# A row of transfers in another order: exchange a pair ahead, two pairs fetched into room of late outputs, the second pair first (hash attention and feed-forward, one core)

## The chip, the cores and the metric

The kernel runs on one core of a Trainium2 chip. The core has TensorE (PE) for matrix products, VectorE (DVE), ScalarE (ACT) and GpSimd (POOL) for elementwise work, and SyncE (SP), which here only issues transfers (DMA). All share an on-chip memory, SBUF; PE writes its sums to PSUM. The metric is the device time of one execution in microseconds (us), the median of several; less is better.

## The reference

Two blocks follow one another. The first is attention in which a query sees only keys with the same hash; the second is a feed-forward with a GELU.

```python
# q, k, v: (4, 8, 768, 64) f32; proj: (64, 6); x: (3072, 512); w_in: (512, 2048); w_out: (2048, 512)
q_bits = (np.einsum('bhsd,dk->bhsk', q, proj) > 0)       # 6 bits; the same for k
mask = q_bucket[:, :, :, None] == k_bucket[:, :, None, :]
scores = np.where(mask, scale * np.matmul(q, k.transpose(0, 1, 3, 2)), -1e9)
attn = softmax(scores)                                    # rows
x = np.matmul(attn, v)  -> (B*S, H*D)
h = x @ w_in
out = (h * (1.0 / (1.0 + np.exp(-1.702 * h)))) @ w_out
```

## The kernel before, in words

**Tiling of the attention.** Two heads of one batch make a *pair*; there are 16 pairs (0 to 15). A head has 64 columns, so a pair fills 128 partitions. The 768 queries are halved (c = 0, 1; 384 each), and the 768 keys are six tiles of 128 (kt). For a half and a key tile PE makes scores in a PSUM place (`place`, four of them in turn, `in_turn`), ACT writes their exponentials into `es[c]` (`weigh`, L486), POOL and DVE add them up over the key tiles (`add_low`, L525, into one shared `low_sum`; `add_high`, L535 and L538), and PE multiplies them with the values (`values`, L547). ACT moves that into `xT` (`unload`, L558 and L559), and two half-pairs later DVE multiplies by the inverse of the sums (`total` on PE, L569; `invert`; `norm`, L590).

**The mask.** It is no comparison but a second term in the scores. `hashed` (L461) multiplies keys and queries with the projection, DVE writes one tile `f` of signed bits (`featured`, L466), and eight transfers (two of them from ACT in pair 1) bring its parts of 16 rows into the feature tile `feats` of the pair (two tiles, used in turn). Score terms are thus: features, in bf16, and keys by queries in f32.

**Two forms of the score product.** Pairs 0 to 2 (`n < BY_PARTS`, 3) use `scores` (L497): for each key tile and head a product over 64 rows for each term. Later pairs use `scores_of_four` (L514): four products over 32 rows run side by side, for two key tiles and two heads. That needs, beside the pair's own keys and queries (`own`, three in turn), a copy with the 32-row halves of each head exchanged (`other`, written by the four transfers of `exchange`), and the features twice, 32 rows apart (two transfers inside the feature tile). `spread` issues these six.

**Loading.** `fetch` brings keys or queries of a pair into one tile each (`ld` pool, one buffer of each name), in four transfers of 32 partitions, so that a 32 by 32 transposition on DVE (`turn`, L437) makes `own` of it. `measure` (L451) takes the sum of squares of the raw tile on ACT. A fetch of a later pair can start only when both have read the tile. `fetch_v` brings values in two transfers, with two buffers. Pair 0 is special (`first_pair`): loaded by SP and ACT, transposed by PE, with its bits taken by products of their own (L416, L417).

**What sets the order.** The lists of PE, DVE, ACT and POOL run as written. All transfers above are issued by SP, which works its list in order (its rows bear L340, the line of `load`): a transfer that waits holds up all behind it. Up to pair 1 a scheduler may place SP's transfers; from pair 2 on (`turns_kept`) they, too, keep the written order. ACT issues the chunks of w_in (one for each pair from 2 on, `begin`, L165), which DVE and ACT convert in steps (`step`). Behind pair 15 the feed-forward begins (L905, L973, L1232).

The order of a middle pair n on SP is: eight feature transfers of pair n+1, four of `exchange(n + 1)`, two inside the feature tile, four keys of pair n+3, two values of n+1, four queries of n+3:

```python
whole(features)
if n + 1 >= BY_PARTS:
    spread(n + 1)
...
fetch(n + 3, "k")     # behind turn(n + 2, "k") and measure(n + 2, "k")
fetch_v(n + 1)
...
fetch(n + 3, "q")     # behind turn(n + 2, "q") and measure(n + 2, "q")
```

Of the kernel before, what the change touches and what calls it, by code (L numbers as in the profile page):

```python
# [19 lines left out]
P = 128  # L20
# [18 lines left out]
def kernel(  # L39
# [249 lines left out]
    def attention(ff):  # L289
# [4 lines left out]
        with actx:  # L294
# [34 lines left out]
            BY_PARTS = 3  # L329
# [7 lines left out]
            turns_kept = [False]  # L337

            def load(out, in_):
                dma = nc.sync.dma_start(out=out, in_=in_)  # L340
                if turns_kept[0]:
                    tc.keep_in_program_order(dma)
                return dma
# [6 lines left out]
            def behind(x):  # L350

                nc.vector.memset(x, 0.0)
# [14 lines left out]
            def fetch_v(n):  # L367
                b, hp = pairs[n]
                x = ld.tile([P, T, 2, D], F32, tag="v", name="v", bufs=2)
                if n == 0:  # L370
                    x = x.rearrange("p t j d -> p (t j d)").rearrange("p (j t d) -> p t j d", j=2, d=D)
                vts[n] = x
                if n == 1:
                    behind(x[:, 0, :, 0])
                for j in range(2):
                    order = "(t p) d -> p t d" if n else "(p t) d -> p t d"
                    load(x[:, :, j, :], v[b, 2 * hp + j].rearrange(order, p=P))

            def first_pair():
# [16 lines left out]
                for _ in range(4):  # L396
                    nc.tensor.matmul(warm[:, 0], idle[:, 0:P], idle, start=True, stop=True)
# [15 lines left out]
                def bits(name, c, slots=None):  # L413
                    cols = slice(c * HS, (c + 1) * HS)
                    h = (place(slots.pop(0)) if slots else in_turn())[:, 0, 0:HS]
                    nc.tensor.matmul(h, pf0[name].rearrange("p j d -> p (j d)"), xts[0, name][:, cols], start=True, stop=True)  # L416
                    nc.vector.tensor_scalar(feats[0][name][:, cols], h, above0[name][:, 0:1], FEAT[name],  # L417
                                            op0=Alu.is_gt, op1=Alu.mult)
# [60 lines left out]
            def spread(n):  # L479

                exchange(n)
# [6 lines left out]
            def scores(n, c, kts, slots=None):  # L488
                qT, kT, qf, kf = xts[n, "q"], xts[n, "k"], feats[n % 2]["q"], feats[n % 2]["k"]
                cols = slice(c * HS, (c + 1) * HS)  # L490
                for kt in kts:
                    ps = in_turn() if slots is None else place(slots.pop(0))
                    keys = slice(kt * P, (kt + 1) * P)
                    for a, m, last in ((kf, qf, False), (kT, qT, True)):
                        for j in range(2):
                            hs = slice(D * j, D * (j + 1))
                            nc.tensor.matmul(ps[:, j, 0:HS], a[hs, keys], m[hs, cols], start=not last, stop=last)  # L497
                    weigh(n, c, kt, ps)

            def scores_of_four(n, groups):  # L500

                for c, k0 in groups:
# [6 lines left out]
                    for at, (a, m) in enumerate(((f["k"], f["q"]), (x[:, 0], x[:, 1]), (y[:, 0], y[:, 1]))):  # L509
# [30 lines left out]
            def values(n, c, kts, at):  # L540
                av, vt = at[:, 0 : HS + 1], vts[n]
                avs[n, c] = av
                for t in kts:
                    row = t if n else 2 * (t % GT) + t // GT
                    for j in range(2):
                        for d in range(0, D, 32):
                            nc.tensor.matmul(av[D * j + d : D * j + d + 32, :], vt[:, row, j, d : d + 32], es[c][:, t, j, :],  # L547
# [44 lines left out]
            last = len(pairs) - 1  # L592
# [29 lines left out]
            scores(0, 0, low, slots)  # L622
            rest(slots)
            add_low(0, 0)
            scores(0, 0, high, slots)
            turn(1, "k")
            measure(1, "k")
            values(0, 0, low, at[:, 0])
            fetch(2, "k")
            scores(0, 1, low, slots)  # L630
            turn(1, "q")
# [877 lines left out]
```

## Time and profile before

| what | us |
|---|---|
| median of 3 runs | 855.31 (854.36 to 855.37) |
| the profiled execution, its own time | 857.29 |
| its span, first to last instruction | 855.5 |
| attention, to the first product of the feed-forward | 0 to 317.4 |
| ACT busy with exponentials (192) | 143.7 |
| PE busy with products by the values (1536) | 131.6 |

The rows of the profile name the line, the engine, the operation and the tiles it writes and reads, `out<-in`; in a timeline the first number is the start and the second the length in us, xN is how many instructions are merged in the row, and brackets give the idle time before it and what ended it. A queue's own rows (SPq, ACTq) are issues of transfers; their length includes what the issue waited for. "Landing" is from the issue of a transfer to its end.

### The profile page before, as it was taken

The numbers are of one execution on the slowest core, as the hardware profiler recorded it, in microseconds if no ns is written. First come the engines' busy times: TensorE is split into PE (matmuls) and PEld (weight loads), VectorE is DVE, ScalarE is ACT, GpSimd is POOL, SyncE is SP. The second block draws the span as 40 slices with busy tenths as digits, with TensorE's granted clock in tenths as the row PEclk, the third lists the DMA queues.
The fourth block names the chain that finished last, engine by engine and source line by source line (L and its number), as shares of the span: only waits on it lengthen the run. The fifth ranks groups of instructions, "written<-read, shape, count | busy, mean of one in ns | idle before, by whom it ended". The sixth has DMA issues, their size and how long they took to land.

```text
span 855.5 us, 14892 instructions
## 1 busy us (share of the span) xinstructions
PE 843.9 (99%) x5595; PEld 524.7 (61%) x5595; DVE 683.9 (80%) x1069; ACT 337.6 (39%) x553; POOL 361.8 (42%) x321
## 2 busy tenths in 40 slices
PE   8999999999999999999999999999999999999997
PEld 4444444444444444565666666545888888888886
DVE  4479889988878986788887788676998977897786
ACT  6666665667666644343444444433000000000000
POOL 4333343433433448997854467568664100000000
PEclk9999999999999999999999999999999999999999
DMA  5657866776777403526466546577854675467534
GB/s 112 98 91 150 152 137 134 158 138 130 155 146 142 114 3 135 161 81 264 188 230 221 214 155 213 205 265 269 278 174 154 205 244 194 157 222 233 193 120 100
DMA packets 165197, 144.04 MB, mean 168 GB/s; under 512 B 124384, under 2 KB 139872, under 8 KB 159872
## 3 DMA queue, kind: packets, MB, share of 16 engines
q1 hardware_dynamic: 154640, 111.22, 47.6%
q10 hardware_dynamic: 10480, 31.81, 11.8%
q8 instruction: 45, 0.74, 0.4%
q14 instruction: 32, 0.26, 0.1%
HBM read 79.69 MB, written 50.33 MB: 152 GB/s over the span
## 4 chain that ended last, share of the span: by engine, by line
PE 89%; SPq 3%; DMA 3%; ACT 1%; DVE 1%; issue 1%; POOL 1%; ACTq 0%; DVEq 0%; POOLq 0%
PE product L1232 30%; PE product L905 23%; PE s L547 12%; PE s L514 12%; PE small L973 6%; SPq L340 3%; PE product L973 3%; DMA feat<-feat 1%; PE s L497 1%; DMA q<-in_q_dram 1%; ACT e L486 1%; PE s L569 1%; PE s L461 1%; DVE acc L538 0%; POOL above L334 0%
## 5 line engine op out<-in xcount | busy, mean ns | idle before, releaser
L486 ACT ACTIVATE e<-s 128x768 f32<-128x768 f32 x192 | 143.7, 812 | 62.2 <-PE s L514 46.6
L547 PE MATMUL s<-e,v 128*32 128x385 f32 x1536 | 131.6, 488 | 0.0
L525 POOL TENSOR_TENSOR t_x<-e 128x768 f32<-128x768 f32 x32 | 55.2, 1724 | 137.5 <-ACT e L486 132.0
L905 PE MATMUL product<-xT,w_in_sb 128*128 128x512 f32 x216 | 100.0, 593 | 0.1
L547 PEld LDWEIGHTS s<-e,v 128*32 128x32 f32 x1536 | 47.2, 109 | 79.1 <-issue 60.3
L905 PE MATMUL product<-t_x,s_in 128*128 128x512 f32 x192 | 89.5, 593 | 0.0
L514 PE MATMUL s<-s_in 32*128 32x384 f32 x816 | 79.9, 482 | 0.0
L525 POOL TENSOR_TENSOR t_x<-t_x,e 128x768 f32<-128x768 f32 x32 | 55.9, 1747 | 55.7 <-ACT e L486 54.6
L538 DVE TENSOR_TENSOR acc<-acc,e 128x768 f32<-128x768 f32 x63 | 73.6, 1168 | 2.8 <-ACT e L486 0.6
L1268 ACT COPY u<-product 128x256 f32<-128x256 f32 x20 | 7.4, 372 | 158.1 <-PE product L1232 124.9
L905 PEld LDWEIGHTS product<-xT,w_in_sb 128*128 128x128 f32 x216 | 41.0, 190 | 35.7 <-issue 32.7
L905 PEld LDWEIGHTS product<-t_x,s_in 128*128 128x128 f32 x192 | 36.5, 191 | 29.8 <-issue 26.7
L514 PEld LDWEIGHTS s<-s_in 32*128 32x128 f32 x816 | 41.1, 185 | 19.8 <-issue 1.9
L514 PE MATMUL s<-own 32*128 32x384 f32 x432 | 45.6, 487 | 0.0
L921 DVE TENSOR_TENSOR u<-product,u 128x256 f32<-128x256 f32 (+1 forms) x60 | 28.4, 486 | 15.5 <-PE product L973 12.9
L466 DVE TENSOR_SCALAR f<-s,above,weight 128x384 bf16<-128x384 f32 x15 | 10.1, 676 | 32.9 <-PE s L569 25.0
L1232 PE MATMUL product<-raw_g,xT 128*128 128x256 f32 x152 | 35.1, 380 | 0.0
L514 PE MATMUL s<-feat 32*128 32x384 bf16 x312 | 30.4, 327 | 2.5 <-DMA feat<-feat 2.0
L226 POOL TENSOR_TENSOR v<-c,v 128x1024 f32<-128x1024 f32 (+1 forms) x15 | 32.3, 2156 | 1.0
L225 POOL TENSOR_TENSOR u<-v,u 128x1024 f32<-128x1024 f32 (+1 forms) x11 | 23.8, 2166 | 20.2 <-ACT v L918 14.1
L921 DVE TENSOR_TENSOR v<-product,v 128x512 f32<-128x512 f32 x24 | 16.5, 689 | 19.5 <-PE product L905 19.5
L535 DVE SCALAR_TENSOR_TENSOR acc<-t_x,e 128x768 f32<-128x768 f32 x31 | 29.4, 947 | 3.1 <-ACT e L486 2.5
(298 smaller groups left out, 1801.1 us busy)
## 6 DMA issues: line engine op xcount, KB each, us to landing
raw_g<-g_dram SPq DMA_DIRECT2D x20, 1024.0 KB, 5.1
s_in<-g_dram SPq DMA_DIRECT2D x20, 1024.0 KB, 5.0
g_dram<-c ACTq DMA_DIRECT2D x18, 512.0 KB, 2.9
raw<-in_moe_w_out_dram ACTq DMA_DIRECT2D x16, 512.0 KB, 3.7
raw<-in_moe_w_in_dram ACTq DMA_DIRECT2D x15, 512.0 KB, 5.2
s_in<-own SPq DMA_DIRECT2D x36, 192.0 KB, 3.3
v<-in_v_dram SPq DMA_DIRECT2D x32, 192.0 KB, 3.8
k<-in_k_dram SPq DMA_DIRECT2D x60, 96.0 KB, 3.1
```

Source lines behind the costliest of these rows:

```text
L226: lambda: eng.tensor_tensor(b12, b22, b12, op=Alu.subtract),
L340: dma = nc.sync.dma_start(out=out, in_=in_)
L486: nc.scalar.activation(es[c][:, kt, :, 0:HS], ps[:, :, 0:HS], Act.Exp, scale=1.0 / D**0.5)
L514: nc.tensor.matmul(ps[i][:, j, 0:HS], a[r0 : r0 + 32, keys], m[r0 : r0 + 32, cols], start=at == 0, stop=at == 2)
L525: nc.gpsimd.tensor_tensor(low_sum, low_sum if i else e[:, 0], e[:, i + 1], op=Alu.add)
L535: nc.vector.scalar_tensor_tensor(acc, terms[0], T * TINY, terms[1], op0=Alu.add, op1=Alu.add)
L538: nc.vector.tensor_tensor(acc, acc, terms[i + 1], op=Alu.add)
L547: nc.tensor.matmul(av[D * j + d : D * j + d + 32, :], vt[:, row, j, d : d + 32], es[c][:, t, j, :], start=(t == 0), stop=(t == T - 1))
L905: nc.tensor.matmul(ps, wq[LEFT[i]][:, kc, :], xq[RIGHT[i]][:, kc, :], start=(start and kc == 0), stop=(kc == K2 - 1), skip_group_check=not ...
L921: nc.vector.tensor_tensor(dst, x, y, op=Alu.add)
L973: nc.tensor.matmul(x, wq[LEFT[i]], xq[RIGHT[i]], start=start, stop=True, skip_group_check=True)
L1232: nc.tensor.matmul(ps, wq[LEFT[i]][:, c, :], gq[RIGHT[i]][:, c, :], start=(onto is None and c == 0), stop=(c == F4 - 1), skip_group_check= ...
```

## The change

- **Row of a middle pair on SP.** `exchange` leaves `spread`, which becomes `copied` (the two transfers inside the feature tile). For pair n+2 (not n+1) it is issued at the end of pair n's row, behind the query fetch. `copied(n + 1)` comes behind the key fetch and ahead of the values. Values are one transfer (tile order p, j, t, d; was p, t, j, d). All of SP's transfers keep the written order from the start.
- **Room.** Keys and queries of pairs 1 and 3 are fetched into the parts of `xT` that pairs 14 and 13 write at their end, instead of into the tiles of the `ld` pool.
- **Forms.** `BY_PARTS` is 2: pair 2 also has 32-row products. Pair 0's scores begin with the f32 term.
- **Pairs 0 and 1.** One more warm-up product. In `first_pair` the second halves' bits come behind the first three key tiles, as one piece (`second`). The fetches of pairs 1, 2, 3 and 4 come earlier, and the values of pair 0 behind the fetch of pair 1. The hash of pair 2 and the sums of pair 0 (`total`) come ahead of pair 1's scores, and its features right behind; pair 1 leaves the loop and is written out: all scores of its first half, all of its second, then the values of the first.

```diff
-            BY_PARTS = 3
+            BY_PARTS = 2
...
             def load(out, in_):
-                dma = nc.sync.dma_start(out=out, in_=in_)
-                if turns_kept[0]:
-                    tc.keep_in_program_order(dma)
-                return dma
+                return tc.keep_in_program_order(nc.sync.dma_start(out=out, in_=in_))
...
                 b, hp = pairs[n]
-                x = raws[n, name] = ld.tile([P, S // 32, 32], F32, tag=name, name=name)
-                if (n, name) == (2, "q"):
-                    behind(x[:, 0, 0:1])
+                if n in (1, 3):
+
+                    b1, hp1 = pairs[last - 1 - "kq".index(name)]
+                    x = xT[:, hp1, b1 * S : (b1 + 1) * S].rearrange("p (s i) -> p s i", i=32)
+                else:
+                    x = ld.tile([P, S // 32, 32], F32, tag=name, name=name)
+                raws[n, name] = x
...
-                x = ld.tile([P, T, 2, D], F32, tag="v", name="v", bufs=2)
+                x = vts[n] = ld.tile([P, 2, T, D], F32, tag="v", name="v", bufs=2)
+                heads = v[b, 2 * hp : 2 * hp + 2]
+                if n:
+                    load(x.rearrange("p j t d -> p (j t) d"), heads.rearrange("j (t p) d -> p (j t) d", p=P))
...
-                for _ in range(4):
+                for _ in range(5):
...
                 placed("k", tk, 0, (act, act))
                 tq = turned("q")
+                placed("q", tq, 0, (act, dve))
+                bits("k", 0, in_turn()[:, 0])()
                 placed("k", tk, 1, (act, dve))
-                placed("q", tq, 0, (act, dve))
-                bits("k", 0)
-                bits("q", 0)
-                measure(0, "k")
-                placed("q", tq, 1, (act, act))
-                bits("k", 1)
-                measure(0, "q")
-                return lambda slots: bits("q", 1, slots)
+                bits("q", 0, in_turn()[:, 0])()
+                placed("q", tq, 1, (act, dve))
+
+                def second():
+                    at = place(3)
+                    for f in [bits(x, 1, at[:, i]) for i, x in enumerate("kq")]:
+                        f()
+
+                return second
...
-            def spread(n):
-
-                exchange(n)
+            def copied(n):
+
                 for j in range(2):
                     load(both[n % 2][D * j + 32 : D * j + 48], both[n % 2][D * j : D * j + 16])
...
             rest = first_pair()
-            fetch_v(0)
             for x in "kq":
                 fetch(1, x)
+            fetch_v(0)
             slots = [2, 0, 1] * 5
+            scores(0, 0, low, slots)
+            measure(0, "k")
+            fetch(2, "k")
+            rest()
+            measure(0, "q")
+            fetch(2, "q")
+            add_low(0, 0)
...
+            fetch_v(1)
+            for x in "kq":
+                fetch(3, x)
             scores(0, 1, low, slots)
...
             whole(featured(1))
-            fetch(2, "q")
-            fetch_v(1)
             scores(0, 1, high, slots)
-            measure(2, "k")
+            for x in "kq":
+                turn(2, x)
+                measure(2, x)
+            exchange(2)
+            add_high(0, 1)
             at = place(3)
             values(0, 1, every, at[:, 0])
+            hashed(2, at[:, 1])
             unload(0, 1)
-            turns[0] = 0
-            inverse = {}
-            for n in range(1, last + 1):
+            at = place(0)
+            total(0, at[:, 0])
+            turns[0] = 1
+
+            features = featured(2)
+            next(features)
+            inverse = {0: invert(0)}
+            next(inverse[0])
+            whole(features)
+            for x in "kq":
+                fetch(4, x)
+            scores_of_four(1, ((0, 0), (0, 2), (0, 4)))
+            add_low(1, 0)
+            copied(2)
+            for x in "kq":
+                turn(3, x)
+            fetch_v(2)
+            exchange(3)
+            add_high(1, 0, (0, 1))
+            next(inverse[0])
+            scores_of_four(1, ((1, 0), (1, 2), (1, 4)))
...
+            for x in "kq":
+                measure(3, x)
+            at = in_turn()
+            values(1, 0, every, at[:, 0])
+            hashed(3, at[:, 1])
+            unload(1, 0)
+            for n in range(2, last + 1):
...
+                if n + 3 <= last:
+                    fetch(n + 3, "k")
                 if n < last:
+                    copied(n + 1)
                     fetch_v(n + 1)
...
                 if more:
-                    measure(n + 2, "k" if n == 1 else "q")
-                    if n > 1 and n + 3 <= last:
+                    measure(n + 2, "q")
+                    if n + 3 <= last:
                         fetch(n + 3, "q")
+                    exchange(n + 2)
```

More of the change, by code (lines that the diff above doesn't have):

```diff
@@ new lines, in attention @@
+            add_high(1, 0, (0, 1))
+            next(inverse[0])
+            scores_of_four(1, ((1, 0), (1, 2), (1, 4)))
+            add_low(1, 1)
+            norm(0)
+            add_high(1, 0, (2,))
+            for x in "kq":
+                measure(3, x)
[4 more added lines that the diff above has]
+            for n in range(2, last + 1):
+                more = n + 2 <= last
+                if n == last:
+                    turns[0] += 1
+                if n < last:
+                    features = featured(n + 1)
+                    next(features)
+                if n > 2:
+                    inverse[n - 2] = invert(n - 2)
+                    next(inverse[n - 2])
+                    step(n - 1, 2 if n == last else 1)
+                scores_of_four(n, ((0, 0),))
+                chunk = begin(n)
+                if n < last:
+                    first = next(features)
+                    if chunk is not None:
+                        behind_issue(chunk, first)
+                        behind_issue(next(features), chunk)
+                    whole(features)
+                scores_of_four(n, ((0, 2),))
@@ L689, in attention @@
                 add_high(n - 1, 1, (2,))
[L690 removed]
+                if n > 2:
                     norm(n - 2)
[L692 to L705 removed]
+                if more:
+                    measure(n + 2, "k")
@@ L713, in attention @@
                 add_high(n, 0, (1,))
-                if n > 1 and more:
+                if more:
                     turn(n + 2, "q")
-                elif n + 1 == last:
+                elif n < last:
                     x_sums[1]()
```

118 lines of the change are left out of this document (26 added, 92 removed).

## Prediction

> **What bounds the kernel now.** I read the page's first and fourth parts first, then the busy time of each pair's stretch, and last the timeline of SyncE (SP) around the longest wait of TensorE (PE).
>
> ```profile
> span 855.5 us, 14892 instructions
> PE 843.9 (99%) x5595; PEld 524.7 (61%) x5595; DVE 683.9 (80%) x1069; ACT 337.6 (39%) x553; POOL 361.8 (42%) x321
> PE 89%; SPq 3%; DMA 3%; ACT 1%; DVE 1%; issue 1%; POOL 1%; ACTq 0%; DVEq 0%; POOLq 0%
> ```
>
> PE is the bound: 99% busy, and 89% of the chain that ended last. What the chain has beside PE is mostly SP and transfers, 3% each. A PE row that is held up still counts as busy, so the page's busy time understates the waits; the length of a pair shows them better. I took each pair from its first score product to that of the next (pair 1 starts at 29.55, pair 2 at 45.96, pair 3 at 66.62, pair 12 at 239.16):
>
> ```profile
> 29.55:45.96 16.41, 16.41 (x149) 8.64 (x146) 9.63 (x10) 12.48 (x20) 6.47 (x4) 1.00 0.80 124
> 45.96:66.62 20.66, 20.07 (x188) 8.78 (x185) 17.22 (x20) 13.35 (x24) 6.58 (x4) 1.00 0.60 116
> 66.62:85.94 19.32, 19.17 (x236) 8.69 (x232) 17.12 (x25) 12.45 (x21) 6.77 (x4) 1.00 0.78 144
> ...
> 142.17:163.37 21.20, 19.18 (x236) 8.79 (x234) 18.33 (x24) 12.57 (x22) 6.91 (x4) 1.00 0.72 142
> ...
> 220.64:239.16 18.52, 18.52 (x237) 8.27 (x234) 15.55 (x23) 12.66 (x22) 7.28 (x4) 1.00 0.76 148
> 239.16:257.68 18.52, 18.52 (x237) 8.29 (x234) 15.54 (x23) 12.60 (x22) 7.26 (x4) 1.00 0.73 144
> ```
>
> After the stretch its length, then the busy time of PE, PE's weight loads, DVE (VectorE), ACT (ScalarE) and POOL (GpSimd). Pairs 11 and 12, which do all of a middle pair's work, take 18.52 with PE busy throughout: that is PE's own pace. The nine pairs from 66.62 to 239.16 took 172.54; at that pace they would take 9 x 18.52 = 166.68. So 5.9 us are lost there, and 2.1 more in pair 2 (20.66 against 18.52). The row of SP around the worst start, that of pair 7 at 142.17:
>
> ```profile
> 121.57 2.33 SPq L340 DMA_DIRECT2D k<-in_k_dram  x4
> 124.00 2.85 SPq L340 DMA_DIRECT2D v<-in_v_dram  x2
> 126.99 2.31 SPq L340 DMA_DIRECT2D q<-in_q_dram  x4
> 129.71 8.76 SPq L340 DMA_DIRECT2D feat<-f  x8
> 138.51 2.49 SPq L340 DMA_DIRECT2D s_in<-own  x4
> 141.12 1.53 SPq L340 DMA_DIRECT2D feat<-feat  x2
> ...
> 123.44 0.68 DVE L466 TENSOR_SCALAR f<-s,above,weight 128x384 bf16<-128x384 f32 x1 [2.65 <-PE s L569]
> 142.17 0.33 PE L514 MATMUL s<-feat 32*128 32x384 bf16 x2
> 144.52 0.67 PE L514 MATMUL s<-feat 32*128 32x384 bf16 x2 [2.02 <-DMA feat<-feat]
> ```
>
> The features were in `f` at 124.1, but their transfers stood behind keys, values and queries of a later pair until 129.71, and the copy inside the tile behind those and the exchange until 142.65, when the pair that needs it had begun (the longest wait of PE, 2.02, is for it). SP has hardly a gap in this row; it is late because what is wanted first comes last.
>
> **The change part by part.** *Row of the middle pairs.* It becomes: eight features, four keys, two copies, one values transfer (was two), four queries, four exchange; the exchange is now that of a pair later. 23 issues instead of 24; a key fetch's row gives 2.33 / 4 = 0.58 us an issue. When each can go follows from the undisturbed pair at 239.16, whose DVE, ACT and POOL lists the change leaves as they are:
>
> ```profile
> 239.29 0.68 DVE L466 TENSOR_SCALAR f<-s,above,weight 128x384 bf16<-128x384 f32 x1 [2.65 <-PE s L569]
> 241.07 0.33 ACTq L165 DMA_DIRECT2D raw<-in_moe_w_in_dram  x1
> 245.07 0.94 DVE L437 STREAM_TRANSPOSE s_in<-k 128x768 f32<-128x768 f32 x1
> 251.52 0.97 DVE L437 STREAM_TRANSPOSE s_in<-q 128x768 f32<-128x768 f32 x1
> raw<-in_moe_w_in_dram ACTq DMA_DIRECT2D x15, 512.0 KB, 5.2
> feat<-feat SPq DMA_DIRECT2D x26, 48.0 KB, 3.2
> DMA to landing us min/median/max: 1.7/3.0/6.2
> ```
>
> From the pair's start: features 0.8 to 5.4. The key fetch needs the key tile transposed (6.9) and, in the built program, where a transfer waits for the one eight places before it, the w_in chunk landed (issue done at 2.2, plus 5.2: 7.4): 7.4 to 9.7. Copies to 10.9, landed at 14.1 (3.2 each): 4.4 before the next pair's 18.52. Behind them values to 11.5; queries need their transpose (13.3): to 15.6; exchange to 17.9, 1.4 before the next `f` at 19.3 (18.52 + 0.8). The next features are the ones queued behind a late query fetch, and 4.4 us lie between them and PE. So the loss should go: -5.9. Bounds: nothing saved (0), all of it (-5.9); I take all, because pairs 11 and 12 show that no other engine holds the pace.
>
> *Pair 2 in parts.* Its scores now use 32-row products with the exchanged halves (12 products for two key tiles, was 8):
>
> ```profile
> 54.50 0.34 PE L497 MATMUL s<-feat 64*128 64x384 bf16 x2
> 56.13 0.33 PE L497 MATMUL s<-feat 64*128 64x384 bf16 x2
> 74.46 0.34 PE L514 MATMUL s<-feat 32*128 32x384 bf16 x4
> 75.93 0.33 PE L514 MATMUL s<-feat 32*128 32x384 bf16 x4
> ```
>
> Two key tiles take 1.63 the old way and 1.47 the new: 6 x 0.16 = 0.96 us saved; the other 1.2 of the 2.1 are its waits for features that came too late. Together -2.1; bounds -1.0 (waits return) and -2.1.
>
> *The beginning.* The pair-1 keys and queries go into `xT` rooms that hold nothing yet, so they need not wait for the first tiles; values come after them. Bits are taken twice before the first scores instead of three times, and first scores begin with the dot product; the other two bits follow three key tiles later (was one). One more warm-up product lies before keys arrive (four took 1.89 from 1.27, five end near 3.6; the first transposition starts at 3.67). Two small memsets on DVE fall away.
>
> ```profile
> 1.27 1.89 PE L397 MATMUL s<-idle 128*128 128x512 bf16 x4 [1.27 <-DVE idle L76]
> 3.67 1.51 PE L406 MATMUL s<-ident,k 128*128 128x128 f32 x6 [0.51 <-DMA k<-in_k_dram]
> 9.66 0.34 PE L497 MATMUL s<-feat 64*128 64x384 bf16 x2
> 12.19 0.91 PE L416 MATMUL s<-own,pf_q 128*128 128x384 f32 x2
> 22.15 0.49 PE L461 MATMUL s<-own,pf_q 128*32 128x384 f32 x2
> 22.47 0.49 PE L461 MATMUL s<-own,pf_q 128*32 128x384 f32 x2
> 23.22 0.94 ACT L559 ACTIVATE xT<-s,vs 128x384 f32<-128x384 f32 x1
> 24.20 0.68 DVE L466 TENSOR_SCALAR f<-s,above,weight 128x384 bf16<-128x384 f32 x1 [4.92 <-ACT xT L559]
> ```
>
> One bit product (0.9 by the row at 12.19) leaves the stretch before 9.66 and returns behind the third key tile. The first scores can begin with the dot product meanwhile, but they end only with the feature product, for which DVE must have written the bits of both first halves, as before; so I take 0.2 of the 0.9 as gained (bounds 0 and 0.9). From there to pair 2 PE has the same work in another order, and pair 1's old stretch had no wait (16.41 of 16.41 busy): PE could start pair 2 at 45.96 - 0.2 = 45.8. SP must get there too. The pair-2 hash now follows the last values of pair 0, ending near 29.55 - 0.2 + 0.8 = 30.1 (the pair-1 hash ran from 22.15 to 22.96); from its end to that of `f`, behind ACT's move of the values, took 24.88 - 22.96 = 1.9; then eight features, eight fetches for pair 4 and two copies, 18 x 0.58 = 10.4; landing 3.2: 45.6. The two meet, so I cost the beginning at 0. Cover is gone there: whatever delays SP is paid at once. Bounds: -0.9 (PE first, all of the bit product gained), and a 6.2 landing instead of 3.2, 48.7 against 45.96, +2.7.
>
> *Others at nothing.* The `measure` steps that move on ACT in pairs 0 to 3 lie beside PE's values and scores: ACT has 16.41 - 12.48 = 3.9 free in the old pair 1. Without that room they would hold back the exponentials, and those the place in PSUM for PE's next scores. Merging the values transfer moves the same bytes with one issue less. Pair 12 has no loss left to remove, and behind the attention every engine's list is as it was.
>
> Sum: -5.9 - 2.1 + 0 = -8.0. The profiled execution took 857.29 (its span 855.5), 2 us over the median 855.31; I take the difference from both: span 847.5, median **847.3**.
>
> **The rivals.** *The copy stays late.* It still stands behind a key fetch that waits for ACT and DVE. Then only the cheaper products remain: 855.3 - 1.0 = 854.3. For it: landings up to 6.2. Against: 4.4 us to spare. Chance 0.12.
>
> *The beginning pays.* Features or copies of pairs 1 and 2 land late and PE waits up to 2.7: 847.3 + 2.7 = 850.0. For: the two estimates meet within 0.2 us, and 18 issues stand between the hash and the copy's landing. Against: a landing of 6.2 is the longest of all, twice the median. Chance 0.18.
>
> *DVE and POOL collide, and it gets slower.* An addition on DVE beside one on POOL was longer:
>
> ```profile
> 135.91 2.30 DVE L538 TENSOR_TENSOR acc<-acc,e 128x768 f32<-128x768 f32 x1
> 135.47 1.92 POOL L525 TENSOR_TENSOR t_x<-e 128x768 f32<-128x768 f32 x1 [4.65 <-ACT e L486]
> 242.01 0.96 DVE L538 TENSOR_TENSOR acc<-acc,e 128x768 f32<-128x768 f32 x1
> ```
>
> 2.30 against 0.96: 1.35 lost each time. DVE has 15.55 to do in 18.52, so it decides from more than (18.52 - 15.55) / 1.35 = 2.2 collisions a pair: with three, 15.55 + 4.05 = 19.6, 1.1 over PE's pace in each of pairs 2 to 13, 12 x 1.1 = 13: 860. For: the change shifts every phase of the pairs. Against: the worst pair had DVE at 18.33, and undisturbed pairs show 15.55. Chance 0.06. [...]
>
> **How the numbers follow.** My forecast has 0.64, the beginning 0.18, the late copy 0.12, the collisions 0.06. The runs shown spread over 1.0 us (854.36 to 855.37). The forecast's own range takes that play to both sides; downward also the beginning's other bound (0.9), upward as much for a single late pair: 845.5 to 849. The beginning's 850.0 with the same 1.0 gives 851 at the top; late copy and collisions are left out, 0.18. About 0.2% (1.7 us) is what a measurement can tell from no change, so within means 853.6 to 857.0. Faster takes forecast, beginning and a third of late copy: 0.86; same the rest, 0.07; slower the collisions and a little, 0.07.
>
> **What would show it.** Pairs 2 to 11 should each last 18.5; SP's features should begin within 1 us of `f`, its copies end some 11 us after the pair's start, with PE's wait for `feat<-feat` gone; pair 2 starts at 45.5 to 46.5 with 32-row products; DVE shows 15.6 a pair. Wrong if pair 2 starts after 47, if the pairs still vary above 18.7, or if SP's row passes the next `f`.

## The result, and the profile after

| | before | after |
|---|---|---|
| median in us | 854.63 (852.03 to 856.64, 8 runs) | 858.54 (856.97 to 859.05, 8 runs) |
| the profiled execution, its own time | 857.29 | 857.87 |
| its span | 855.5 | 856.1 |
| start of pair 2, of pair 3 | 45.96, 66.62 | 46.74, 70.73 |
| pairs 3 to 11 together | 172.54 | 166.66 |
| pair 12 to the first product of the feed-forward (at 317.24 and 316.17) | 78.08 | 78.78 |

The change made the kernel slower: ratio 1.0046, 95% interval 1.0030 to 1.0061, that is 3.9 us, or 0.5%. Forecast were 8.0 us less. The page of the kernel after, first and fourth parts:

```profile
span 856.1 us, 14954 instructions
PE 841.2 (98%) x5644; PEld 522.2 (61%) x5644; DVE 672.1 (79%) x1068; ACT 337.5 (39%) x552; POOL 364.8 (43%) x321
PE 87%; POOL 6%; DVE 2%; ACT 1%; issue 1%; DMA 1%; SPq 0%; ACTq 0%; DVEq 0%; POOLq 0%
```

SP has left the chain of waits (3% before, 0% now), as hoped, and PE's busy time fell by 2.7. The stretches show where the rest is, in the columns of the prediction (pairs 2, 3 and 11):

```profile
46.74:70.73 23.99, 20.66 (x236) 9.52 (x233) 12.42 (x14) 13.12 (x23) 6.76 (x4) 0.93 0.78 162
70.73:89.25 18.52, 18.52 (x236) 8.28 (x233) 15.55 (x23) 12.62 (x22) 7.30 (x4) 1.00 0.69 145
...
218.88:237.39 18.51, 18.51 (x236) 8.25 (x233) 15.54 (x23) 12.61 (x22) 7.29 (x4) 1.00 0.67 142
```

All nine middle pairs take 18.52 (to 0.01), which the prediction expected. But pair 2 takes 23.99, at a mean granted clock of 0.93. The timeline of the kernel after, from SP's third fetch to the wait of pair 2 (rows by queue and engine, not in order of time):

```profile
19.35 7.79 SPq L340 DMA_DIRECT2D xT<-in_k_dram  x4
27.48 2.12 SPq L340 DMA_DIRECT2D xT<-in_q_dram  x4
29.71 3.74 SPq L340 DMA_DIRECT2D feat<-f  x6
33.55 3.08 SPq L340 DMA_DIRECT2D s_in<-s_in  x4
36.72 5.36 SPq L340 DMA_DIRECT2D feat<-f  x8
42.19 2.23 SPq L340 DMA_DIRECT2D k<-in_k_dram  x4
44.51 3.55 SPq L340 DMA_DIRECT2D q<-in_q_dram  x4
48.10 1.16 SPq L340 DMA_DIRECT2D feat<-feat  x2
...
24.24 0.68 DVE L463 TENSOR_SCALAR f<-s,above,weight 128x384 bf16<-128x384 f32 x1 [5.45 <-ACT xT L557]
25.00 1.25 ACTq L472 DMA_DIRECT2D feat<-f  x2
31.51 0.68 DVE L463 TENSOR_SCALAR f<-s,above,weight 128x384 bf16<-128x384 f32 x1 [1.21 <-ACT xT L557]
50.40 0.98 PE L512 MATMUL s<-feat 32*128 32x384 bf16 x2 [3.33 <-DMA feat<-feat]
```

The features of pair 1 are in `f` at 24.92, and the six that SP issues leave from 29.71 on; those of pair 2 are there at 32.19 and leave from 36.72 on; the copies are issued from 48.10 to 49.26, behind the eight transfers that fetch pair 4. PE begins pair 2 at 46.74 with the first two of four products side by side, and then waits 3.33. What follows the wait, in slices of 2 us, and then the stretch at the lower clock by itself (columns as above; the granted clock stands behind POOL):

```profile
48.00:50.00 2.00, 0.00 (x0) 0.00 (x0) 1.97 (x3) 0.00 (x0) 0.00 (x0) 1.00 0.78 135
50.00:52.00 2.00, 1.60 (x10) 1.04 (x14) 1.94 (x3) 0.00 (x0) 0.00 (x0) 0.55 0.88 199
52.00:54.00 2.00, 2.00 (x21) 1.29 (x20) 0.00 (x0) 0.08 (x1) 0.00 (x0) 0.60 1.13 254
54.00:56.00 2.00, 2.00 (x29) 0.93 (x25) 0.00 (x0) 2.00 (x3) 0.49 (x1) 1.00 0.95 209
...
50.21:53.61 3.40, 3.21 (x18) 1.94 (x22) 1.73 (x3) 0.00 (x0) 0.00 (x0) 0.50 1.03 232
```

The wait is paid twice: for 3.4 us behind it the granted clock is 0.50, which by the last row costs (1 - 0.50) x 3.21 = 1.6. Pair 2 is 23.99 - 18.52 = 5.5 over PE's pace. From its first two products to the next two go 3.7 (46.74 to 50.40); from there the next group of products begins at 53.61, 3.21 later, where two key tiles take 1.47 at full clock: 1.7 more.

### The profile page after: what moved, and what is told of

Its sections match the earlier page's. It is cut to its first block, busy times and chain, and to the rows that moved or that the text cites. A ratio compares the mean times of both kernels' runs of the same rounds, so it can differ in the third digit from the quotient of the medians.

```text
span 856.1 us, 14954 instructions
## 1 busy us (share of the span) xinstructions
PE 841.2 (98%) x5644; PEld 522.2 (61%) x5644; DVE 672.1 (79%) x1068; ACT 337.5 (39%) x552; POOL 364.8 (43%) x321
## 3 DMA queue, kind: packets, MB, share of 16 engines
q10 hardware_dynamic: 10480, 31.81, 11.1%
## 4 chain that ended last, share of the span: by engine, by line
PE 87%; POOL 6%; DVE 2%; ACT 1%; issue 1%; DMA 1%; SPq 0%; ACTq 0%; DVEq 0%; POOLq 0%
PE product L1238 30%; PE product L911 16%; PE s L512 15%; PE s L545 14%; PE small L979 5%; PE product L979 2%; PE s L494 2%; PE s L458 1%; PE s L567 1%; ACT e L482 1%; DMA g_dram<-u 1%; POOL c L227 1%; POOL v L226 1%; POOL u L225 1%; POOL w_in_sb L218 0%
## 5 line engine op out<-in xcount | busy, mean ns | idle before, releaser
L523 POOL TENSOR_TENSOR t_x<-e 128x768 f32<-128x768 f32 x32 | 59.2, 1849 | 145.6 <-ACT e L482 145.6
L512 PE MATMUL s<-s_in 32*128 32x384 f32 x912 | 89.3, 488 | 0.0
L523 POOL TENSOR_TENSOR t_x<-t_x,e 128x768 f32<-128x768 f32 x32 | 54.6, 1705 | 43.8 <-ACT e L482 42.4
L536 DVE TENSOR_TENSOR acc<-acc,e 128x768 f32<-128x768 f32 x63 | 67.8, 1076 | 2.1
L512 PEld LDWEIGHTS s<-s_in 32*128 32x128 f32 x912 | 44.8, 187 | 23.7 <-issue 2.9
L512 PEld LDWEIGHTS <-feat 32*128 32x128 bf16 x336 | 10.3, 92 | 38.1 <-issue 26.2
```

Source lines behind the costliest of these rows:

```text
L512: nc.tensor.matmul(ps[i][:, j, 0:HS], a[r0 : r0 + 32, keys], m[r0 : r0 + 32, cols], start=at == 0, stop=at == 2)
L523: nc.gpsimd.tensor_tensor(low_sum, low_sum if i else e[:, 0], e[:, i + 1], op=Alu.add)
L536: nc.vector.tensor_tensor(acc, acc, terms[i + 1], op=Alu.add)
```

## The experiments

Below, *lag* is the time from a pair's first score product to SP's first feature transfer of that pair's row, and *loss* what pairs 3 to 11 took over 9 x 18.52 (times in us). Both come from the timelines. Each ratio is to the kernel before on the same chip; e1 to e4 share a chip and its runs of before, and so do e5 to e8, e9 and e10, e11 and e12, e13 and e14.

| kernel | median (or one time) | ratio to before, interval | start of pair 3 | lag of pairs 3, 4, 5, 6 | loss |
|---|---|---|---|---|---|
| before, the profiled execution | 857.29 | | 66.62 | 5.3, 4.9, 4.1, 6.4 | 5.9 |
| e4, before again | 854.26 | | 66.31 | 4.7, 4.5, 4.4, 6.4 | 1.9 |
| after | 858.54 | 1.0046 (1.0030 to 1.0061) | 70.73 | 0.8 each | 0.0 |
| e5, after again | 858.57 | 1.0042 (1.0022 to 1.0063) | 71.65 | 0.8 each | 0.0 |
| e1 | 855.90 | 0.9987 (0.9967 to 1.0007) | 69.58 | 0.8 each | 0.0 |
| e2 | 856.16 | 1.0002 (0.9982 to 1.0021) | 66.90 | 6.2, 3.8, 3.7, 2.9 | 0.7 |
| e3 | 857.81 | 1.0019 (0.9997 to 1.0041) | 69.50 | 1.2, 0.8, 0.8, 0.8 | 0.0 |
| e6 | 851.58 | 0.9975 (0.9957 to 0.9992) | 64.36 | 4.2, 3.7, 3.6, 2.9 | 0.0 |
| e7 | 850.78 | 0.9946 (0.9926 to 0.9966) | 64.20 | 6.4, 4.8, 3.3, 2.8 | 1.5 |
| e8 | 859.84 | | 73.35 | 0.8 each | 0.0 |
| e9 | 851.18 | 0.9968 (0.9946 to 0.9990) | 64.24 | 2.7, 2.1, 1.4, 0.8 | 0.2 |
| e10 | 862.70 | | 71.93 | 0.8, 2.0, 1.8, 2.1 | 3.1 |
| e11 | 864.76 | 1.0065 (1.0030 to 1.0099) | 67.65 | 5.0, 5.6, 7.6, 7.1 | 11.1 |
| e12 | 852.84 | 0.9949 (0.9922 to 0.9976) | 65.54 | 2.4, 1.4, 0.8, 0.8 | 0.6 |
| e13 | 851.03 | 0.9951 (0.9928 to 0.9973) | 64.14 | 1.2, 0.9, 0.8, 0.8 | 0.0 |
| e14 | 854.04 | | 66.16 | 5.6, 4.8, 4.4, 1.5 | 2.0 |

### What holds SP up at the beginning: e1, e2, e3, e6

Two theories. In the first, SP is held at 19.35 (a fetch of 7.79) by the two transfers that ACT issues for pair 1, since in the built program a transfer waits for the one eight places before it: in the trace of the kernel after the fourth of the four key transfers goes at 26.83, and the first transfer of ACT, eight places before it, landed at 26.81. In the second, the row itself is too long. e1 takes the two transfers from ACT:

```diff
-                            if (n, x, c) == (1, "q", 0):
-                                nc.scalar.dma_start(out=to, in_=of)
-                            else:
-                                yield load(to, of)
+                            yield load(to, of)
```

> Changed kernel with ACT's two feature transfers of pair 1 issued by SP instead. Theory A (hold): in the changed kernel SP's key fetch for pair 3 waits until ACT's feature transfers of pair 1 have landed (7.79 us for four issues that else take 2.3), because both use the same completion slots; the row behind it is late by some 5 us, so that pair 2 waits 3.3 us for its copy. Then here the four key issues take under 3 us, the features of pair 1 begin near 25 and those of pair 2 near 32.3 (was 36.7), the copy of pair 2 is issued by 43 and pair 2 starts without a wait of over 1 us: some 852 (858.5 less 0.7 at pair 1, 3.7 of wait and 1.8 of slow clock). Theory B (depth): the copy is late because 18 issues stand between the hash and it, whatever is ahead; then the wait stays at 2 us or more and the time at 856 or more.

The timeline of e1:

```profile
19.77 3.68 SPq L340 DMA_DIRECT2D xT<-in_k_dram  x4
...
26.34 5.00 SPq L340 DMA_DIRECT2D feat<-f  x8
...
34.68 5.38 SPq L340 DMA_DIRECT2D feat<-f  x8
...
44.89 2.85 SPq L340 DMA_DIRECT2D feat<-feat  x2
...
48.69 0.33 PE L509 MATMUL s<-feat 32*128 32x384 bf16 x1 [2.89 <-DMA feat<-feat]
```

The hold is gone (7.79 to 3.68; in SP's list of waits the longest for `feat<-f` falls from 5.2 to 0.9), the features of pair 1 leave 3.4 earlier, and pairs 1 and 2 start 1.2 and 1.3 earlier. But the copies are still behind the eight transfers of pair 4's fetch, and since PE comes earlier too it waits nearly as long. So the hold was real, but the 852 of the first theory did not come (855.90). e2 leaves the hold and moves the copies:

```diff
             whole(features)
+            copied(2)
             for x in "kq":
                 fetch(4, x)
             scores_of_four(1, ((0, 0), (0, 2), (0, 4)))
             add_low(1, 0)
-            copied(2)
```

> Changed kernel with the two copies of pair 2 ahead of the fetch of pair 4 on SP instead of behind it; ACT's transfers stay. Theory A (hold): the hold of 5 us stays, features of pair 2 still end near 42, but the copies need no longer wait for eight fetches (5.9 us): they land near 47, PE waits 0.5 instead of 3.3, and its clock keeps full: some 853.5. Theory B (depth): the same or better, 853. A rival on both (the wait is not what costs): 857 or more.

No wait of pair 2 for `feat<-feat` is left, pair 2 takes 19.76 (its longest wait, 0.57, is for `xT` on ACT), and pair 3 starts 3.8 earlier than in the kernel after. Pairs 3 and 4 then lose 0.75. The stretches of e2 (pairs 3 and 5), and in its timeline a DVE addition beside one of POOL:

```profile
66.90:86.01 19.11, 18.98 (x236) 8.49 (x233) 18.76 (x25) 12.48 (x22) 7.52 (x4) 1.00 0.80 157
...
104.69:123.21 18.52, 18.52 (x236) 8.27 (x234) 15.55 (x23) 12.69 (x22) 7.64 (x5) 1.00 0.83 158
```

```profile
79.65 2.30 DVE L536 TENSOR_TENSOR acc<-acc,e 128x768 f32<-128x768 f32 x1
...
79.31 1.82 POOL L523 TENSOR_TENSOR t_x<-e 128x768 f32<-128x768 f32 x1 [4.19 <-ACT e L482]
```

DVE is at 18.76 of 19.11 there: the collisions of the third rival exist (this addition took 2.30, the next of its kind, at 82.76 with no POOL instruction beside it, 0.91), but they go away again by pair 5. e3 asks what the clock costs: seven products of zeros fill PE's wait.

```diff
             hashed(3, at[:, 1])
+            filler = in_turn()
+            turns[0] -= 1
+            for _ in range(7):
+                nc.tensor.matmul(filler[:, 0], idle[:, 0:P], idle, start=True, stop=True)
             unload(1, 0)
```

> Changed kernel with seven bf16 products on the idle tile put between the hash of pair 3 and the first scores of pair 2 (about 7 x 0.22 to 0.43 = 1.5 to 3 us of PE's waiting time filled); the copy lands as late as before. Theory C (clock): the 1.8 us that the first two score groups of pair 2 take longer (granted clock 0.5 for 3 us behind a wait of 3.3) come from PE standing still, so they go: 856.7, and the clock stays 1.0 from 46 to 56. Rival: they come from the late exchange or the landing transfers; then the groups stay slow and the time stays 858.5.

The timeline of e3 and the slice behind its wait:

```profile
47.42 1.68 PE L683 MATMUL s<-idle 128*128 128x512 bf16 x7
...
50.49 0.33 PE L512 MATMUL s<-feat 32*128 32x384 bf16 x1 [0.99 <-DMA feat<-feat]
```

```profile
52.00:54.00 2.00, 2.00 (x28) 1.08 (x21) 0.63 (x1) 1.31 (x2) 0.00 (x0) 1.00 1.21 254
```

With a wait of 0.99 the clock stays at 1.00. From the end of the wait to pair 3 it is 19.01 (50.49 to 69.50) instead of 20.33 (50.40 to 70.73): 1.3 of pair 2's 5.5 were the clock by this run, 1.6 by the granted clock above. (Pairs 1 and 2 together take 36.64 instead of 38.56; the other 0.6 of that is pair 1, which began 0.7 later here while the copies left at nearly the same time.) The medians are too close to show it by themselves: the intervals of the two ratios, 1.0019 and 1.0046, overlap. e6 makes both edits of SP's row, beside the kernel after once more (e5):

> The kernel after, unchanged, so that the variants share a chip with it. If the 3.9 us are a steady property of its beginning, pair 1 starts at 32.2, pair 2 at 46.7 and waits some 3 us for feat<-feat with a granted clock of 0.5 to 0.6 behind the wait, pair 3 starts at 70 to 71, pairs 3 to 11 take 18.52 each, and the time is 1 to 4 us above the kernel before on this chip. If the wait was an accident of one execution, pair 3 starts before 68 and the time is that of before.

> Both edits of SP's row together: the features of pair 1 all from SP, and the copies of pair 2 ahead of pair 4's fetches. Theory (two separate delays of SP, the hold by ACT's transfers and the copies behind eight fetches, add up): pair 1 starts at 31.0, pair 2 at 45.5, no wait above 0.5 us for feat<-feat and a clock of 1.00 there, pair 2 takes 18.5 to 19.8, pair 3 starts at 64.0 to 65.3 (after 70.7, copies first alone 66.9); time 4 to 6 us below the kernel after of the same call. Rival (DVE and POOL, not SP: what PE no longer waits for at pair 2 it loses in pairs 3 to 5, where DVE was at 18.8 of 19.1 with the copies first): pair 3 starts at 64 to 65.3, but pairs 3 to 5 lose 2 us or more, and the time is only 2 to 3 us below the kernel after.

e5 repeats the kernel after on another chip: 858.57, with a wait of 3.2. The stretches of e6 (pairs 2 and 3):

```profile
45.62:64.36 18.74, 18.74 (x237) 8.31 (x235) 12.15 (x14) 13.22 (x23) 7.82 (x4) 1.00 0.78 160
64.36:82.87 18.51, 18.51 (x236) 8.26 (x232) 15.64 (x23) 12.61 (x22) 7.45 (x4) 1.00 0.77 145
```

Pair 2 has lost 5.25 of its 23.99, and the median is 7.0 below e5's, 1.0 more than the theory's upper figure. Both delays of SP were real; the copies' place is the larger, and either edit alone left PE or DVE waiting.

### The end of the attention: e7

```diff
-                if n == last:
-
-                    turns[0] += 1
```

(beside e6's edits)

> The same two edits, and without the place that is skipped at the last pair. Theory (the skipped place makes PE wait 0.36 for ACT at the start of pair 15 and costs 0.7 in pairs 14 and 15): that wait goes, pair 14 takes 17.9, from pair 15's start to the first product of the feed-forward 23.2 (23.66 with the turn), time 0.5 to 0.9 below the kernel with both edits. Rival (without the turn another place is still being read: ACT's wait moves or grows): pairs 14 and 15 together take as long or up to 1 us longer.

PE's rows at the start of pair 15, e6 and then e7:

```profile
286.83 0.34 PE L509 MATMUL s<-feat 32*128 32x384 bf16 x2 [0.36 <-ACT e L479]
```

```profile
287.26 0.54 PE L509 MATMUL s<-feat 32*128 32x384 bf16 x4
```

The place that is skipped at the last pair costs 0.7: pair 14 takes 17.87 instead of 18.08, and from pair 15 to the feed-forward it is 23.16 instead of 23.67. The median fell by 0.8. (In its profiled execution pairs 3 to 5 lost 1.5, which e6's had not.)

### Why the middle pairs are steady: e8 to e14

The prediction gave the loss of the middle pairs to the order of SP's row. e8 puts the old order back (the kernel after otherwise):

```diff
                     whole(features)
+                    if n > 2:
+                        exchange(n + 1)
+                    copied(n + 1)
...
-                    copied(n + 1)
                     fetch_v(n + 1)
...
-                    exchange(n + 2)
```

> The kernel after with the row of the middle pairs as before: exchange of the next pair and the copies behind the features, then keys, values, queries. Beginning as in the kernel after. Theory (the row keeps the middle pairs at PE's pace): pairs 3 to 11 lose 1.9 to 6 us again over 9 x 18.52, with waits for feat<-feat or feat<-f of up to 2 us. Rival (the pairs are steady for another reason, as the values in one transfer or where DVE's and ACT's work falls): pairs 3 to 11 keep 18.52 to 18.6 each.

The rival held: the old order keeps 18.52 as well. In e8 PE's wait in pair 2 (2.9) may have let SP catch up first, so e9 takes the same rows with e6's edits, without that wait:

> Both edits of the beginning, and the middle pairs' row on SP as before (exchange of the next pair and the copies behind the features, then keys, values, queries). Theory (the old row keeps the middle pairs at 18.52 only where PE's long wait in pair 2 has let SP catch up first; without that wait the row stays 4 to 6 us behind `f`, ACT's w_in transfer waits for the keys issued late, and exponentials and additions come late): pairs 3 to 11 lose 2 to 6 us over 9 x 18.52, the w_in transfer is issued 3 to 5 us after a pair's start (1.9 in the kernel after), and the time is 2 to 6 us above the kernel with both edits. Rival (the order of the row is nothing; one transfer fewer for the values is enough to catch up): pairs 3 to 5 lose 1 us at most, from pair 6 on 18.52, time within 1 us of the kernel with both edits.

The rival again: the lag starts at 2.7 and drains, the loss is 0.2, and the time is that of e6. So the order of the row isn't what the middle pairs need. e4, another execution of the kernel before, profiled beside e1 to e3, shows what goes wrong in it:

> The kernel before once more, for a second profile. Its timed runs have a median 2.7 us under its profiled execution. Theory D: the profiled execution had a larger loss in the middle pairs than usual (5.9 us over PE's pace); here pairs 3 to 11 lose 2 to 4 us and the time is 852 to 856. Rival: the loss in the middle pairs is 5 to 6 us again, and the difference lies elsewhere.

It lost only 1.9. Its stretches of pairs 6 and 11, and PE's and the weight load's first rows of pair 6, with a clean first row from pair 5 at 103.84:

```profile
122.35:141.40 19.05, 19.05 (x237) 8.70 (x235) 17.45 (x23) 12.67 (x22) 6.68 (x4) 1.00 0.73 147
216.36:234.87 18.51, 18.51 (x236) 8.25 (x233) 15.55 (x23) 12.67 (x22) 7.29 (x4) 1.00 0.63 132
```

```profile
103.84 0.34 PE L514 MATMUL s<-feat 32*128 32x384 bf16 x4
...
122.35 0.87 PE L514 MATMUL s<-feat 32*128 32x384 bf16 x4
...
122.89 0.09 PEld L514 LDWEIGHTS <-feat 32*128 32x128 bf16 x1 [0.24 <-DMA feat<-feat]
```

Half a microsecond is lost at the first product, for copies that come late (they landed at 122.51 and 122.84): small waits inside a busy row of PE. PE's list of waits has 2.0 for `feat<-feat` in the whole execution of before; the weight load's has more, in pairs 3 to 11 of before (us in total, times, longest):

```profile
PEld L514 <- DMA feat<-feat: 4.4, 8, 2.3
```

By place, 5.5 of the 5.9 that the profiled execution of before lost lie between a pair's first score products and its second group. In e4 it is 1.1 of 1.9. DVE's higher sum in such a pair comes from additions that then run beside POOL's (2.06 and 2.30 in pair 6). e10 asks whether ACT, whose w_in transfer is issued late in these pairs (4.9 behind the start of pair 6, 1.9 in the kernel after), is a second way to lose:

```diff
                         behind_issue(next(features), chunk)
+                        if 3 <= n <= 11:
+                            junk = xT[:, HP - 1, (B - 1) * S : (B - 1) * S + 512]
+                            for _ in range(4):
+                                nc.scalar.activation(junk, idle, Act.Square)
```

> The kernel after with four more ACT instructions (the square of a tile of zeros, 128x512, some 0.55 to 0.65 us each, into a place written anew later) right behind the w_in transfer in pairs 3 to 11: ACT is held there some 2.4 us, as it was in the kernel before where that transfer waited. Theory (it is ACT, held at that transfer, through which a late row costs PE): what was free is from 1.9 to about 3.1 us, so pairs 3 to 11 lose 0.4 to 1.5 us each, 18.9 to 20.0, with POOL's first addition 0.3 to 1.3 us later (3.33 in the kernel after) and some additions on DVE of 1.6 to 2.3 us; SP's features still begin 0.8 us after the pair's start. Rival (the pairs before lost by late features and copies alone, and ACT has room for 2.4 us): pairs 3 to 11 stay at 18.52 to 18.6.

The timeline of e10 in pair 6 and just ahead of it, the stretch of pair 6, and from the weight load's list of waits in pairs 3 to 11:

```profile
131.50 2.62 ACT L704 ACTIVATE xT<-idle 128x512 f32<-128x512 bf16 x4
...
126.61 1.89 POOL L523 TENSOR_TENSOR t_x<-t_x,e 128x768 f32<-128x768 f32 x1 [3.40 <-ACT e L482]
...
126.99 2.07 DVE L200 TENSOR_TENSOR w_in_sb<-bits,w_in_sb 128x512 f32<-128x512 f32 x1
...
130.19 0.09 PEld L512 LDWEIGHTS <-feat 32*128 32x128 bf16 x2 [0.58 <-DVE rt L573]
```

```profile
128.37:147.25 18.88, 18.84 (x237) 8.38 (x234) 18.57 (x24) 15.00 (x26) 7.44 (x5) 1.00 0.62 137
```

```profile
PEld L512 <- DVE rt L573: 4.6, 8, 0.6
```

2.62 of ACT cost 0.2 to 0.4 a pair, where the theory had 0.4 to 1.5, and by another way: POOL's second addition is 1.3 later, in most pairs three instructions of DVE run beside one of POOL's (1.9 to 2.1 instead of 0.7 to 1.0), DVE is nearly full (18.57 of 18.88), and it comes late to `rt`, for which PE's second group of scores waits. Over nine pairs that is 3.1, more than e4 lost in all; it is the place that tells the two apart. In e10 nothing is lost at a pair's first products, where before lost 5.5 of its 5.9. Of e4's 1.9 some 0.7 (pairs 3 and 9) lie where e10's do, so ACT held may be a second, smaller way.

e11 and e12 ask for the number of transfers: values in one transfer in the kernel before (e11), and in two in e9's kernel (e12):

```diff
 e11
-                for j in range(2):
-                    order = "(t p) d -> p t d" if n else "(p t) d -> p t d"
-                    load(x[:, :, j, :], v[b, 2 * hp + j].rearrange(order, p=P))
+                if n:
+                    load(x.rearrange("p j t d -> p (j t) d"), heads.rearrange("j (t p) d -> p (j t) d", p=P))
...
 e12
-                    load(x.rearrange("p j t d -> p (j t) d"), heads.rearrange("j (t p) d -> p (j t) d", p=P))
+                    for j in range(2):
+                        load(x[:, j], heads[j].rearrange("(t p) d -> p t d", p=P))
```

> The kernel before with one edit of the change alone: the values of a pair in one transfer instead of two (tile order p, j, t, d), 23 transfers of SP in a middle pair instead of 24. Theory (the old row with 24 is as long as a pair, so that SP never catches up; with 23 it does): SP's features come earlier from pair to pair, the w_in transfer goes to 1.9 to 2.9 us after a pair's start, pairs 3 to 11 lose at most 1 us over 9 x 18.52, and the time is 1 to 4 us below the kernel before. Rival (the pairs before lose by something that the beginning or the forms of the products bring, not by the number of transfers): features stay 4 to 8 us behind the pair's start, pairs 3 to 11 lose 1.9 to 6 us, time within 1 us of the kernel before.

> The kernel with both edits and the old row, now with the values in two transfers too, so that SP's row of a middle pair is wholly that of the kernel before (24 transfers). Theory (with 24 SP never catches up): features 3 to 8 us behind the pair's start through pairs 3 to 11, w_in transfer at 2.5 us or later, pairs 3 to 11 lose 1.9 to 6 us, time 1.5 to 6 us above the same kernel with one transfer. Rival (24 catch up as well): pairs 3 to 11 lose at most 1 us, time within 1 us of it.

Both theories fell. With one transfer less (and the tile's order p, j, t, d, which came with it) the kernel before is slower (864.76, loss 11.1, nine waits of up to 1.8 for `feat<-feat`), and with one more e9's kernel still drains its lag (2.4, 1.4, 0.8). One worse stretch of e11, pair 9:

```profile
184.69:205.67 20.98, 19.17 (x237) 8.70 (x234) 17.93 (x24) 12.60 (x22) 7.05 (x4) 1.00 0.76 147
```

In the table one thing parts the old rows that stay steady (e8, e9, e12) from those that don't (before, e4, e11): the lag with which they come into pair 3, 2.7 or less against 4.7 or more. Two runs for that. e13 gives e12's kernel the exchange of pair 3 in its old place, in pair 2's row; e14 gives the kernel before two short rows, without the exchange of pairs 6 and 7 (these two pairs are computed with other pairs' halves):

```diff
 e13
                     whole(features)
-                    if n > 2:
-                        exchange(n + 1)
+                    exchange(n + 1)
...
             fetch_v(2)
-            exchange(3)
 e14
-                exchange(n)
+                if n not in (6, 7):
+                    exchange(n)
```

> The kernel of e12 (both edits, old row, values in two transfers) with the exchange of pair 3 back in pair 2's row, so that SP has the whole row of before from pair 2 on. Theory (the old row keeps a lag of 4 us or more once it has it, and needed the lighter row of pair 2 to get below): SP's features start 4 to 6 us after pair 3's start and stay 3 us or more behind through pair 8, pairs 3 to 11 lose 1.9 to 6 us over 9 x 18.52 (e12 lost 0.6), and the time is 1 to 5 us above e12's 852.84. Rival (it drains whatever it starts from): below 1.5 us by pair 7, pairs 3 to 11 lose at most 1.3 us, time within 1 us of e12.

> The kernel before without the exchange of pairs 6 and 7 (eight transfers of SP are left out in the rows of pairs 5 and 6, so these two pairs use another pair's exchanged halves). Theory (the old row holds a small lag as well as a large one): SP's features start under 3 us behind the start of pair 7 and go to 0.8, the w_in transfer of ACT is issued at 1.9, and from pair 8 to pair 12 every pair takes 18.52 to 18.6. Rival (something else in the kernel before, as the forms or the places in PSUM, brings the lag back): within four pairs the features are 4 us or more behind again and two or more of the pairs 8 to 12 take over 18.7.

e13 came in with a lag of 1.2, not the 4 to 6 that its theory wanted, since the four transfers no longer stood ahead of the features that begin pair 2's row; it therefore says nothing of a large lag, but shows that the whole old row serves as well as the new (851.03). e14 decides, in its one execution. Its stretches of pairs 5, 6 and 11, and SP's features in pairs 5 and 7:

```profile
104.63:123.74 19.11, 18.84 (x236) 8.61 (x233) 15.77 (x23) 12.61 (x22) 6.59 (x4) 1.00 0.74 127
123.74:142.26 18.52, 18.52 (x236) 8.28 (x233) 15.55 (x23) 12.65 (x22) 7.32 (x4) 1.00 0.82 128
...
216.33:234.85 18.52, 18.52 (x237) 8.26 (x234) 15.56 (x23) 12.61 (x22) 7.29 (x4) 1.00 0.79 150
```

```profile
109.01 7.60 SPq L340 DMA_DIRECT2D feat<-f  x8
...
143.10 5.79 SPq L340 DMA_DIRECT2D feat<-f  x8
```

The lag is 4.4 in pair 5, 1.5 in pair 6 and 0.84 from pair 7 on, with the whole row back, and pairs 6 to 12 take 18.52 each. The kernel before is steady as soon as SP has once caught up. Behind a fetch that has only just been issued the eight features took 7.60, behind a pause 5.79. My estimate from these two, which no run here tests, is that a late row makes itself longer and so stays late.

## Why the prediction was wrong

- **What bounds the kernel; the loss of the middle pairs.** Right in kind: late copies cost PE most of the time that before lost, the pairs hold 18.52 once they are in time, and all 5.9 of its profiled execution went. Wrong in size: that was one execution. e4 (854.26, near the 854.63 of the result) lost 1.9, and the runs of before went from 851.24 to 863.42. The step "I take the difference from both" carried 4.0 that e4 doesn't have; what the slower runs of before lost in these pairs was not profiled. Wrong in reason: the old order holds 18.52 too once SP enters the middle with a small lag (e8, e9, e13, e14). The new order can drain a larger lag (e7 from 6.4, e2 from 6.2; e6, from 4.2, lost nothing), which the old one was not seen to do from 4.1 or more; with the small lag that the rest of the change brings it is worth nothing that these runs show.
- **The row's times** (features from 0.8, keys from 7.4, exchange to 17.9) hold: SP starts its features at 0.84 and its keys at 6.91 in pairs 3 to 5, and the exchange of pair 3's row ends at 17.98.
- **The beginning, "I cost the beginning at 0".** This is the step that failed. PE's half was right: freed of SP's delays, pair 2 starts at 45.5 (e1) and 45.6 (e6), forecast 45.8. SP's half was too short: "SP must get there too" went from the hash of pair 2 straight to its features, as if SP were idle at 32.0. It had fetches, the features of pair 1 and an exchange to finish and began at 36.72, 4.7 late, part of it by the hold that e1 removed; the 18 issues took 12.5, not 10.4. So the copies were issued by 49.26 instead of 42.4. The bound of +2.7 rested on a longer landing alone, and the landing was no cause: 2.2, where 3.2 was forecast. No term stood for the clock (1.3 to 1.6). Forecast for pair 3's start were 45.96 + 18.52 = 64.5; the kernel after reached 70.73, e6 64.36.
- **Pair 2 in parts.** The products are as forecast: with the copies in time pair 2 takes 18.7 (e6, e13).
- **Others at nothing.** The feed-forward's lists are the same and its stretch varies (538.3 and 539.1 before, 539.9 after). The skipped place was left out: 0.7.
- **The rivals.** "The beginning pays" named the place, but with half the price. Collisions came (e2, e7, e10) and cost tenths (pair 3 of e7 took 19.14, 0.62 over PE's pace), not 1.1 a pair.

Against e4's execution of before (span 852.5) the sum closes: start of pair 3 +4.4, middle -1.9, pair 12 to the feed-forward +0.2, feed-forward +0.9, together 3.6; the spans differ by 3.6.

What stays open: what part of the change lowers SP's lag on entering pair 3 (the fetches into `xT`'s room and the earlier hash are likely, but none was tried alone), and why e11 is worse than before.

Five versions have an interval wholly below 1 against the kernel before: e6, e7, e9, e12 and e13, with ratios from 0.9946 to 0.9975. e7 (850.78) and e13 (851.03) have the lowest medians.

## What to carry to other kernels

Where a queue issues in order, follow its whole list up to the transfer that matters, from the first thing it still owes, and put what an engine wants next ahead of fetches for later pairs. Before an order is blamed for a loss, ask whether the queue would be in time had it once caught up; a little slack at the start can be worth more than a better row in the steady state. And take the gain from several executions of before: here the kernel whose queue runs late scatters, and one profile showed three times the loss of the other.

## What the hardware showed

- **Behind waits of some 3 us the granted clock fell.** In the kernel after, with a wait of 3.33, it was 0.50 from 50.21 to 53.61 and 1.00 from there to 55.00; in e1, with a wait of 2.89, it was 0.60 and 0.54 in the two slices of 2 us from 50.00 to 54.00. Behind the 0.99 of e3 (slices to 54.00) and the 2.02 of before (144.50 to 150.00) it stayed at 1.00. Over a whole profiled execution the mean granted clock was 0.996 in the kernel after, 0.995 in e8, and 0.999 in e6, where PE is busy throughout pair 2 (18.74 of 18.74). What length of wait it takes, these runs show no closer than that.
- **Here a late queue went with a scattered time.** The kernel before, with a lag of 4 us and more, ran from 851.24 to 863.42 beside the experiments; e13, with a lag under 1.3, from 849.75 to 851.77.
